# Two instead of three x tiles transposed on TensorE at the head of a gated attention/MLP kernel, and another order of the first loads

## The chip, the cores and the metric

The kernel runs on one core of a Trainium2 chip. The metric is the device time of one execution in microseconds (us). The engines are TensorE (PE in the profile, its weight loads PEld), VectorE (DVE), ScalarE (ACT), GpSimd (POOL) and SyncE (SP). DMAs are issued by SP, ACT or POOL and carried by 16 DMA engines; each issuing engine has a ring of its own (in the profile q1 holds what SP issued, q10 what ACT issued).

## The reference

```
x = A_x                                     # 1 x 2048 x 512, bf16
qkv = x @ wqkv                              # split into q, k, v; 32 heads of 16
phi(t) = where(t > 0, t + 1, exp(t)) + 1e-6
kv = phi(k)^T v ; z = sum over s of phi(k)  # per head, linear attention
a  = (phi(q) kv / (phi(q) z + 1e-6)) @ wo
h  = layernorm(x)                           # over the 512 features
u  = gelu(h^T w1 + b1)                      # mixes the 2048 tokens, 2048 -> 1792
b  = (u w2 + b2)^T                          # 1792 -> 2048
g  = sigmoid(sum(x * gate_w))               # one gate per token
out = g * a + (1 - g) * b
```

## The kernel before, in words

x is handled as 16 tiles of 128 tokens x 512 features. It is needed in two layouts: `xs` with the tokens on the partitions (plain loads, line 126), and `xT` with the features on the partitions. TensorE multiplies with the contraction on the partitions, so K and Q, which contract over features, need `xT`; the layernorm, the token mixing and the product x^T phi(K) need `xs`.

The work on TensorE comes in stages, and the order on every engine is written out by hand (`manual_schedule`): each engine does its instructions in the order in which the program names them, and waits where an input is not there.

1. Six matmuls on a constant (`warm_up`, tile `wps`).
2. The head: the first `HEADS` tiles of x are transposed on TensorE. `transpose_part` multiplies 128-column pieces of `xs` with an identity matrix into a PSUM bank `pt`, and `copy_part` copies them into `xT` on VectorE (line 212) or ScalarE (line 210). The other tiles come into `xT` by DMA transposes straight from memory (`load_xT`, line 132, issued by SP).
3. K for one tile (`k_part`, tile `kacc`): four matmuls of 512 columns, one for each 128 features, each with one piece of `Wk` (`wk_sb`). Then `k_phi`: ScalarE takes the exponential (line 216), VectorE finishes phi in two instructions (lines 217 and 220) into `pk`.
4. From tile 4 on, K of tile t alternates with `g_tile(t - 4)`: four matmuls into the four banks `gacc`, from `xs` and `pk` of the earlier tile. Layernorm statistics (line 240), their use (line 256) and small loads go between.
5. Token mixing with W1 (`uacc`), interleaved at first with Q (`qacc`), then the attention's small products, then for each output tile `aps` and `yps`, and the store.

W1 arrives in four chunks (`w1c`), W2 later in the same buffers.

What sets the order around the change: SP issues x tile 0, x tile 1, piece 2 of Wk, and then the DMA transposes. Ahead of those stands an instruction on VectorE at line 156 which copies eight columns of `xs` tile 0 into `xT` where the first DMA transpose will write. Its values are overwritten; but the transpose has to wait for it, and it waits for x tile 0. ACT issues the first two pieces of Wk in one load, then x tile 2, then piece 3 of Wk. Each DMA is told of by one of eight semaphores, used in turn; a DMA which takes one over is issued only after its earlier user has landed.

Of the kernel before, what the change touches and what calls it, by code (L numbers as in the profile page):

```python
# [15 lines left out]
def kernel(  # L16
# [13 lines left out]
    nc = tc.nc  # L30
    P = nc.NUM_PARTITIONS
# [8 lines left out]
    NT = S // P  # L40
    ND = D // P
# [15 lines left out]
    w1_view = B_w1.rearrange("(t p) f -> p t f", p=P)  # L57
# [8 lines left out]
    def keep(shape, dtype, name):  # L66
        return persist.tile(shape, dtype, name=name, tag=name)

    def bank(name, dtype=FP32):
        return ps.tile([P, SC], dtype, name=name, tag="bank")  # L70

    xs = keep([P, NT, D], BF16, "xs")
    hs = keep([P, NT, D], BF16, "hs")
    xT = keep([P, ND, S], BF16, "xT")
# [34 lines left out]
    def mm(o, lhsT, rhs, start, stop, **kw):  # L109
        nc.tensor.matmul(o, lhsT=lhsT, rhs=rhs, start=start, stop=stop, **kw)  # L110
# [14 lines left out]
    def load_x(q, t0, n):  # L125
        q.dma_start(out=xs[:, t0 : t0 + n, :], in_=x_view[:, t0 : t0 + n, :])

    def load_wk(q, k, n):
        q.dma_start(out=wk_sb[:, k : k + n, :], in_=wqkv_view[:, k : k + n, D : 2 * D])

    def load_xT(t0, n):
        nc.sync.dma_start(
            out=xT[:, :, t0 * P : (t0 + n) * P], in_=X[t0 * P : (t0 + n) * P, :], transpose=True
        )

    load_x(nc.sync, 0, 1)
    load_wk(nc.scalar, 0, 2)
    load_x(nc.sync, 1, 1)
    load_x(nc.scalar, 2, 1)
    load_wk(nc.sync, 2, 1)  # L140
    load_wk(nc.scalar, 3, 1)
    nc.vector.memset(ones_f[:], 1.0)
    nc.vector.memset(mhalf[:], -0.5)
    nc.gpsimd.memset(ident[:], 0.0)
    nc.gpsimd.affine_select(
        out=ident[:], in_=ident[:], compare_op=ALU.not_equal, fill=1.0, base=0,
# [5 lines left out]
        out=maskQ[:], in_=maskH[:].rearrange("p (a m) -> p m a", m=2), op=ALU.max, axis=AX.X  # L152
    )
    nc.gpsimd.memset(brow[:], 0.0)

    nc.vector.tensor_copy(
        out=xT[:, :, 3 * P : 3 * P + 2],
        in_=xs[:, 0, 0 : 2 * ND].rearrange("p (k c) -> p k c", k=ND),
    )
    load_xT(3, 2)  # L160
    load_xT(5, 3)
    load_x(nc.sync, 3, 1)
    load_x(nc.sync, 4, 4)
    for t0, n in ((8, 4), (12, 4)):
        load_xT(t0, n)
        load_x(nc.sync, t0, n)
# [2 lines left out]
    for c, (j0, nb) in enumerate(w1_chunks):  # L169
        w = wpool.tile([P, NT, FB * P], BF16, name="w1c", tag="wc")  # L170
        w1c.append(w)
        for t0 in range(0, NT, 8) if c == 0 else (0,):
            t1 = t0 + 8 if c == 0 else NT
            nc.sync.dma_start(
                out=w[:, t0:t1, : nb * P], in_=w1_view[:, t0:t1, j0 * P : (j0 + nb) * P]
            )
        if c == 0:
            nc.sync.dma_start(out=wv_sb[:], in_=wqkv_view[:, :, 2 * D : 3 * D])
            nc.sync.dma_start(out=wo_sb[:], in_=wo_view)
# [21 lines left out]
    def transpose_part(t, k0, k1):  # L201
        pt = pts[t, k0, k1] = bank("pt")
        for k in range(k0, k1):
            mm(pt[:, k * P : (k + 1) * P], xs[:, t, k * P : (k + 1) * P], ident[:], True, True)

    def copy_part(t, k0, k1, on_act):
        src = pts.pop((t, k0, k1))[:, k0 * P : k1 * P].rearrange("p (k s) -> p k s", k=k1 - k0)
        dst = xT[:, k0:k1, t * P : (t + 1) * P]
        if on_act:
            nc.scalar.activation(out=dst, in_=src, func=ACT.Copy)  # L210
        else:
            nc.vector.tensor_copy(out=dst, in_=src)

    def phi(dst, acc):
        e = work.tile([P, SC], BF16, name="e", tag="e", bufs=6)
        nc.scalar.activation(out=e[:], in_=acc[:], func=ACT.Exp)  # L216
        nc.vector.tensor_scalar(  # L217
            out=e[:], in0=e[:], scalar1=1.0, scalar2=PHI_EPS, op0=ALU.min, op1=ALU.add
        )
        nc.vector.scalar_tensor_tensor(  # L220
            out=dst, in0=acc[:], scalar=0.0, in1=e[:], op0=ALU.max, op1=ALU.add
        )
# [3 lines left out]
    def k_part(t, ks):  # L226
        if t not in kaccs:
            kaccs[t] = bank("kacc")
        for k in ks:
            mm(  # L230
                kaccs[t][:], xT[:, k, t * P : (t + 1) * P], wk_sb[:, k, :],
                k == 0, k == ND - 1,
            )

    def k_phi(t):
        phi(pk[:, t, :], kaccs.pop(t))
# [46 lines left out]
    def ln_step(u):  # L283
        ln_stats(u)
        if u % TPC == TPC - 1:
            ln_rstd(u // TPC)

    HEADS = 3
    for k0, k1 in ((0, 1), (1, 2), (2, ND)):
        transpose_part(0, k0, k1)  # L290
        copy_part(0, k0, k1, k0 == 2)
    k_part(0, range(2))
    for k0, k1 in ((0, 1), (1, 2), (2, ND)):
        transpose_part(1, k0, k1)
    for k0, k1 in ((0, 2), (2, ND)):
        transpose_part(2, k0, k1)
    copy_part(1, 0, 1, False)
    copy_part(1, 1, 2, True)
    copy_part(2, 0, 2, False)
    copy_part(2, 2, ND, True)  # L300
    copy_part(1, 2, ND, False)
    k_part(1, range(2))
    k_part(2, range(2))
    ln_step(0)
    for t in range(HEADS):
        k_part(t, (2,))
    for t in range(HEADS):
        k_part(t, (3,))
        k_phi(t)
    ln_step(1)  # L310
    LAG = 4
    LN_LAG = 5
    APPLY = 10
    for t in range(HEADS, NT):
        k_part(t, range(ND))
# [144 lines left out]
    for j in range(NB0, NF):  # L460
        c, jj = divmod(j, FB)
# [30 lines left out]
        out=gg[:], in0=gth[:], scalar1=0.5, scalar2=0.5, op0=ALU.mult, op1=ALU.add  # L492
    )
    nc.vector.tensor_scalar(
        out=c1[:], in0=gth[:], scalar1=-0.5, scalar2=0.5, op0=ALU.mult, op1=ALU.add
# [3 lines left out]
    for t in range(NT):  # L499
        c, tl = divmod(t, TPC)  # L500
        aps = bank("aps")
        for j in range(ND):
# [3 lines left out]
            out=a_sc[:], in_=aps[:], func=ACT.Identity,  # L506
            scale=gg[:, t : t + 1], bias=c2[:, t : t + 1],
        )
        for c0, W in ((0, 2 * P), (2 * P, P), (3 * P, P)) if t == NT - 1 else ((0, D),):
            cs = slice(c0, c0 + W)  # L510
            yps = bank("yps")
            for f in range(NF):
# [6 lines left out]
                out=ot[:, :W], in0=yps[:, :W], scalar=c1[:, t : t + 1], in1=a_sc[:, cs],  # L519
# [35 lines left out]
```

## Time and profile before

| | |
|---|---|
| runs, median (lowest to highest) | 162.54 us (162.47 to 163.53) |
| profiled execution, span of its instructions | 160.8 us |
| the same execution's own time | not recorded apart from the span; the median is 1.74 us above the span |
| TensorE busy | 156.3 us, 97% |
| granted TensorE clock after the first 4 us | full, to the end |

The span runs from the first to the last instruction. What lies around it (start and end of the execution) is in the times of the runs and not in the span.

The loads of the head, by the trace: issued, landed (the last completion mark), all in us from the span's start.

| load | issued by | size | issued | landed |
|---|---|---|---|---|
| x tile 0 | SP | 128 KB | 0.81 | 3.23 |
| Wk pieces 0, 1 | ACT | 256 KB | 0.80 | 3.94 |
| x tile 1 | SP | 128 KB | 1.27 | 4.32 |
| x tile 2 | ACT | 128 KB | 1.30 | 4.70 |
| Wk piece 2 | SP | 128 KB | 1.73 | 5.15 |
| Wk piece 3 | ACT | 128 KB | 1.82 | 6.03 |
| xT tiles 3, 4 (transpose) | SP | 256 KB | 3.45 | 7.21 |
| xT tiles 5 to 7 (transpose) | SP | 384 KB | 4.83 | 8.71 |
| x tile 3 | SP | 128 KB | 6.70 | 10.21 |
| x tiles 4 to 7 | SP | 512 KB | 7.32 | 11.60 |
| xT tiles 8 to 11 (transpose) | SP | 512 KB | 7.79 | 13.51 |
| W1 chunk 0, two halves | SP | 2 x 1 MB | 17.04, 19.71 | 26.11, 29.42 |

### The profile page before, as it was taken

Reading aid. Unit: us, or ns where it says so; the run is one execution under the profiler, and the core shown is the slowest. Engines: PE = TensorE matmul, PEld = TensorE weight load, DVE = VectorE, ACT = ScalarE, POOL = GpSimd, SP = SyncE. Lnnn points to the kernel's source line nnn. Section 1 sums busy time; section 2 is a strip of 40 time slices with the busy share of each in tenths; the row PEclk is TensorE's granted clock in tenths of the full one; section 3 lists DMA queues with packets and bytes.
Section 4 is the critical chain, followed back from the end, with each engine's and each line's share of the span. In section 5 each row is a group of like instructions: output and inputs, shape, how many; then the busy total and the mean of one; then the engine's idle time right before and its main releaser. Section 6 shows DMA issues by size and latency. Waiting matters only on the chain.

```text
span 160.8 us, 2241 instructions
## 1 busy us (share of the span) xinstructions
PE 156.3 (97%) x826; PEld 72.6 (45%) x840; DVE 124.8 (78%) x276; ACT 72.8 (45%) x114; POOL 7.3 (5%) x17
## 2 busy tenths in 40 slices
PE   7999999999999999999999999999999999999993
PEld 2444444444444444444444444444444444444462
DVE  1599999769999998756999999676999999711122
ACT  3552476654978483059873330237433442111110
POOL 3000332002020000000000000000000000000000
PEclk9999999999999999999999999999999999999999
DMA  5999999999970007600930689501000001110001
GB/s 165 229 235 238 274 335 295 359 348 348 335 177 0 0 0 236 225 0 5 335 120 2 186 270 288 169 33 37 33 33 33 33 33 60 47 60 33 33 33 33
DMA packets 29369, 22.94 MB, mean 143 GB/s; under 512 B 7824, under 2 KB 29328, under 8 KB 29360
## 3 DMA queue, kind: packets, MB, share of 16 engines
q1 hardware_dynamic: 28400, 21.89, 46.1%
q10 hardware_dynamic: 848, 0.79, 1.4%
q0 software_dynamic: 112, 0.14, 0.7%
q8 instruction: 6, 0.10, 0.3%
q14 instruction: 3, 0.02, 0.0%
HBM read 19.01 MB, written 2.10 MB: 131 GB/s over the span
## 4 chain that ended last, share of the span: by engine, by line
PE 94%; DVE 3%; issue 1%; ACT 0%
PE uacc L110 30%; PE yps L110 30%; PE aps L110 9%; PE qacc L110 8%; PE gacc L110 8%; PE kacc L110 7%; PE wps L110 2%; DVE pk L220 1%; DVE e L217 1%; DVE stats L240 0%; ACT e L216 0%; PE kvps L110 0%; PE pt L110 0%; PE w2ps L110 0%; DVE ot L518 0%
## 5 line engine op out<-in xcount | busy, mean ns | idle before, releaser
L110 PE MATMUL uacc<-hs,w1c 128*128 128x512 bf16 (+1 forms) x230 | 51.2, 379 | 0.3 <-issue 0.2
L110 PE MATMUL yps<-uT,w2c 128*128 128x512 bf16 (+2 forms) x247 | 50.8, 355 | 0.3
L110 PEld LDWEIGHTS <-w2c 128*128 128x128 bf16 x252 | 23.6, 98 | 25.2
L110 PEld LDWEIGHTS <-w1c 128*128 128x128 bf16 (+1 forms) x233 | 21.8, 98 | 26.0 <-issue 0.2
L505 ACT ACTIVATE a_sc<-aps,c,gg 128x512 f32<-128x512 f32 x16 | 12.4, 774 | 31.2 <-PE aps L110 15.5
L518 DVE SCALAR_TENSOR_TENSOR ot<-yps,c,a_sc 128x512 bf16<-128x512 f32 (+2 forms) x18 | 12.3, 688 | 15.4 <-PE yps L110 11.7
L339 ACT ACTIVATE uT<-uacc,bcol 128x512 bf16<-128x512 f32 x14 | 9.3, 686 | 17.5 <-PE uacc L110 17.4
L110 PE MATMUL aps<-W2sb,pqT 128*128 128x512 bf16 x63 | 16.4, 379 | 0.1
L110 PE MATMUL qacc<-xT,wq_sb 128*128 128x512 bf16 x61 | 16.1, 379 | 0.2
L110 PE MATMUL kacc<-wk_sb,xT 128*128 128x512 bf16 x63 | 15.9, 380 | 0.2
L404 DVE STREAM_TRANSPOSE zT<-pz 128x512 f32<-128x512 f32 x16 | 11.3, 705 | 6.0 <-ACT pz L403 6.0
L110 PE MATMUL gacc<-pk,xs 128*128 128x512 bf16 x63 | 15.6, 379 | 0.0
L256 ACT ACTIVATE hs<-xs,nmr,rstd 128x512 bf16<-128x512 bf16 x16 | 12.8, 805 | 2.3 <-DVE nmr L250 2.3
L403 ACT ACTIVATE pz<-pqT,zcol 128x512 f32<-128x512 bf16 x16 | 11.4, 714 | 4.8 <-DVE ot L518 4.7
L216 ACT ACTIVATE e<-kacc 128x512 bf16<-128x512 f32 x16 | 9.2, 596 | 9.7 <-PE kacc L110 9.6
L216 ACT ACTIVATE e<-qacc 128x512 bf16<-128x512 f32 x16 | 9.5, 594 | 7.7 <-PE qacc L110 7.7
L413 DVE STREAM_TRANSPOSE rex<-rd 128x512 bf16<-128x512 bf16 x16 | 11.4, 712 | 0.6
L220 DVE SCALAR_TENSOR_TENSOR pk<-kacc,e 128x512 bf16<-128x512 f32 x16 | 11.1, 692 | 0.6
L220 DVE SCALAR_TENSOR_TENSOR pqT<-qacc,e 128x512 bf16<-128x512 f32 x16 | 11.1, 691 | 0.6
L406 DVE TENSOR_REDUCE den<-zT 128x32 f32<-128x512 f32 x16 | 11.0, 686 | 0.6
L110 PEld LDWEIGHTS <-xs 128*128 128x128 bf16 x76 | 7.2, 100 | 8.3 <-DMA xs<-in_A_x_dram 0.6
L240 DVE BATCH_NORM_STATS2 stats<-xs 128x6 f32<-128x512 bf16 x16 | 10.9, 683 | 0.0
(59 smaller groups left out, 99.3 us busy)
## 6 DMA issues: line engine op xcount, KB each, us to landing
w2c<-in_B_w_dram SPq DMA_DIRECT2D x8, 896.0 KB, 5.8
w1c<-in_B_w_dram SPq DMA_DIRECT2D x2, 2048.0 KB, 15.7
w1c<-in_B_w_dram SPq DMA_DIRECT2D x3, 1024.0 KB, 9.7
out_dram<-ot SPq DMA_DIRECT2D x13, 128.0 KB, 1.7
xs<-in_A_x_dram SPq DMA_DIRECT2D x3, 512.0 KB, 4.5
wq_sb<-in_A_wqkv_dram SPq DMA_DIRECT2D x1, 512.0 KB, 6.6
wv_sb<-in_A_wqkv_dram SPq DMA_DIRECT2D x1, 512.0 KB, 10.4
wo_sb<-in_A_wo_dram SPq DMA_DIRECT2D x1, 512.0 KB, 9.1
```

The source lines that it names most:

```text
L110: nc.tensor.matmul(o, lhsT=lhsT, rhs=rhs, start=start, stop=stop, **kw)
L216: nc.scalar.activation(out=e[:], in_=acc[:], func=ACT.Exp)
L220: nc.vector.scalar_tensor_tensor(out=dst, in0=acc[:], scalar=0.0, in1=e[:], op0=ALU.max, op1=ALU.add)
L240: nc.vector.bn_stats(out=stats[:], in_=xs[:, t, :])
L256: nc.scalar.activation(out=hs[:, t, :], in_=xs[:, t, :], func=ACT.Identity, scale=rstd[:, t : t + 1], bias=nmr[:, t : t + 1],)
L339: nc.scalar.activation(out=uT[:, j, :], in_=acc[:], func=ACT.Gelu_apprx_tanh, bias=bcol[:, j : j + 1])
L403: nc.scalar.activation(out=pz[:], in_=seg, func=ACT.Copy, scale=zcol[:, j : j + 1])
L404: nc.vector.transpose(out=zT[:], in_=pz[:])
L406: nc.vector.tensor_reduce(out=den[:], in_=zT[:].rearrange("p (a d) -> p a d", d=HEAD), op=ALU.add, axis=AX.X)
L413: nc.vector.transpose(out=rex[:].rearrange("p (a d) -> p a d", d=HEAD), in_=rd[:].unsqueeze(2).to_broadcast([P, SC // HEAD, HEAD]),)
L505: nc.scalar.activation(out=a_sc[:], in_=aps[:], func=ACT.Identity, scale=gg[:, t : t + 1], bias=c2[:, t : t + 1],)
L518: nc.vector.scalar_tensor_tensor(out=ot[:, :W], in0=yps[:, :W], scalar=c1[:, t : t + 1], in1=a_sc[:, cs], op0=ALU.mult, op1=ALU.add,)
```

## The change

The head transposes two tiles on TensorE instead of three. Their two loads go first, one on SP's ring and one on ACT's, and Wk follows in four pieces of 128 KB, two on each ring. Behind them on SP stand the DMA transposes of tiles 2 and 3, one tile each, then those of tiles 4 and 5 and of tiles 6 and 7, and then one plain load of tiles 2 to 7. The copy at line 156 is gone, so that no DMA transpose waits for x tile 0 by that way. The first chunk of W1 comes in one load of 2 MB. On TensorE all eight transposes come first, then pieces 0 and 1 of K for both tiles, then pieces 2 and 3; the layernorm statistics of tile 0 come behind phi of both tiles.

```diff
     load_x(nc.sync, 0, 1)
-    load_wk(nc.scalar, 0, 2)
-    load_x(nc.sync, 1, 1)
-    load_x(nc.scalar, 2, 1)
+    load_x(nc.scalar, 1, 1)
+    load_wk(nc.sync, 0, 1)
+    load_wk(nc.scalar, 1, 1)
     load_wk(nc.sync, 2, 1)
     load_wk(nc.scalar, 3, 1)
+    load_xT(2, 1)
+    load_xT(3, 1)
...
-    nc.vector.tensor_copy(
-        out=xT[:, :, 3 * P : 3 * P + 2],
-        in_=xs[:, 0, 0 : 2 * ND].rearrange("p (k c) -> p k c", k=ND),
-    )
-    load_xT(3, 2)
-    load_xT(5, 3)
-    load_x(nc.sync, 3, 1)
-    load_x(nc.sync, 4, 4)
+    load_xT(4, 2)
+    load_xT(6, 2)
+    load_x(nc.sync, 2, 6)
...
-        for t0 in range(0, NT, 8) if c == 0 else (0,):
-            t1 = t0 + 8 if c == 0 else NT
-            nc.sync.dma_start(
-                out=w[:, t0:t1, : nb * P], in_=w1_view[:, t0:t1, j0 * P : (j0 + nb) * P]
-            )
+        nc.sync.dma_start(out=w[:, :, : nb * P], in_=w1_view[:, :, j0 * P : (j0 + nb) * P])
...
-    HEADS = 3
+    HEADS = 2
     for k0, k1 in ((0, 1), (1, 2), (2, ND)):
         transpose_part(0, k0, k1)
-        copy_part(0, k0, k1, k0 == 2)
-    k_part(0, range(2))
-    for k0, k1 in ((0, 1), (1, 2), (2, ND)):
+    for k0, k1 in ((0, 2), (2, ND)):
         transpose_part(1, k0, k1)
-    for k0, k1 in ((0, 2), (2, ND)):
-        transpose_part(2, k0, k1)
-    copy_part(1, 0, 1, False)
-    copy_part(1, 1, 2, True)
-    copy_part(2, 0, 2, False)
-    copy_part(2, 2, ND, True)
+    copy_part(0, 0, 1, False)
+    copy_part(0, 1, 2, True)
+    copy_part(0, 2, ND, False)
+    copy_part(1, 0, 2, True)
     copy_part(1, 2, ND, False)
-    k_part(1, range(2))
-    k_part(2, range(2))
+    for ks in (range(2), range(2, ND)):
+        for t in range(HEADS):
+            k_part(t, ks)
+            if ks[-1] == ND - 1:
+                k_phi(t)
     ln_step(0)
-    for t in range(HEADS):
-        k_part(t, (2,))
-    for t in range(HEADS):
-        k_part(t, (3,))
-        k_phi(t)
     ln_step(1)
```

## The prediction

> **What bounds the kernel.** I read the page first: how busy TensorE is, in which slices, and what the chain that ended last is made of.
>
> ```profile
> span 160.8 us, 2241 instructions
> ...
> PE 156.3 (97%) x826; PEld 72.6 (45%) x840; DVE 124.8 (78%) x276; ACT 72.8 (45%) x114; POOL 7.3 (5%) x17
> ...
> PE   7999999999999999999999999999999999999993
> ...
> PE 94%; DVE 3%; issue 1%; ACT 0%
> ```
>
> TensorE is busy in every slice and is 94% of the chain. Next, the busy time of the engines stage by stage, and the waits of TensorE over the whole run (engine, line, what it waited for, total, times, longest):
>
> ```profile
> 0.84:3.36 2.52, 2.52 (x6) 0.79 (x7) 0.36 (x4) 1.06 (x1) 1.14 (x6) 1.00 0.53 167
> 3.36:4.06 0.70, 0.63 (x6) 0.37 (x5) 0.41 (x3) 0.46 (x3) 0.00 (x0) 1.00 1.13 368
> 4.06:5.13 1.07, 1.07 (x11) 0.73 (x11) 0.49 (x3) 0.63 (x2) 0.00 (x0) 1.00 0.79 259
> 5.13:9.02 3.89, 3.89 (x19) 1.65 (x19) 2.73 (x8) 2.34 (x5) 0.00 (x0) 1.00 1.01 190
> 9.02:32.33 23.31, 23.20 (x107) 10.58 (x108) 21.53 (x54) 12.63 (x21) 3.82 (x5) 1.00 1.08 297
> ```
>
> ```profile
> PE wps L110 <- PEq L539: 0.8, 1, 0.8
> PE uacc L110 <- issue: 0.2, 1, 0.2
> ```
>
> The first number after the window is its length, the second TensorE's busy time: from 5.13 us on they are the same, and no DMA or other engine holds TensorE up. A matmul of 512 columns starts every 0.216 us (18 in the 3.89 us from 5.13). So the end of the kernel is the start of the head plus all work behind it, and the change is worth what it moves the first `g_tile` matmul, which starts at 9.02 now: everything from there on is the same on TensorE. It is moved back only if an input of a later stage comes late.
>
> The head itself, in order of time:
>
> ```profile
> 3.36 0.63 PE L110 MATMUL pt<-ident,xs 128*128 128x128 bf16 x4
> ...
> 4.06 0.62 PE L110 MATMUL kacc<-wk_sb,xT 128*128 128x512 bf16 x2
> 4.52 0.62 PE L110 MATMUL pt<-ident,xs 128*128 128x128 bf16 x8
> 5.13 4.06 PE L110 MATMUL kacc<-wk_sb,xT 128*128 128x512 bf16 x18
> 9.02 1.03 PE L110 MATMUL gacc<-pk,xs 128*128 128x512 bf16 x4
> ```
>
> The 5.66 us from 3.36 to 9.02 are, by starts: 4 transposes at 0.107 us (the array's clock is granted in full only from 4.14), 0.27 us of waiting for the copy into `xT`, 2 K matmuls (0.46), 8 transposes at 0.057 (0.46), 0.15 us for the next copy, and 18 K matmuls (3.89).
>
> **The change on TensorE.** It has 8 transposes and 20 K matmuls before the first `g_tile`. The transposes start at 3.36 as now (behind `wps`; x tile 0 still leads SP's ring). Seven run at 0.107 and one at 0.057, to 4.17. The copies keep their durations: VectorE's first ends at 4.00, ScalarE's 128-column piece (0.28) at 4.11, ScalarE's 256-column piece of tile 1 (0.38) begins when the sixth transpose is through, about 4.24, and ends 4.63. So K starts at 4.20, and the third K matmul waits for that copy, to 4.67 instead of 4.63. Eight head matmuls then end at 4.67 + 6 x 0.216 = 5.97, tiles 2 to 4 at 5.97 + 12 x 0.216 = **8.56**. Without any late load the gain is 9.02 - 8.56 = 0.46 us: only 0.07 of it from transposes (0.88 us for twelve, 0.81 for eight, since seven of them now run before the clock is up), the rest from the waits on copies, 0.42 before and 0.07 now, which other transposes cover.
>
> **The loads.** The landings of before are spaced by bytes, not by ring: 384 KB at 3.94, 512 KB at 4.32, 640 KB at 4.70, 768 KB at 5.15, some 0.37 us for 128 KB. By position the new order gives x tile 1 at about 3.6 (needed 3.79), Wk pieces 0 to 3 at 3.94, 4.32, 4.70 and 5.15; needed at 4.20, 4.42, 5.10 and 5.32. The last is the doubtful one. Wk piece 3 of before, the load which the transposes overtook, had ten of its sixteen completion marks by 5.35 and the last at 6.03, 0.88 behind the load before it and not 0.4. The line-156 copy held the transposes to 3.45; now they are issued from 2.13 and stand directly behind Wk piece 2, while piece 3 is on the other ring. So I take its tail with it: 6.03 less one tile's 0.37 = 5.66. The ends are 5.15 and 6.03. At 5.66, K waits 0.34 us and tile 2 begins at 6.31.
>
> The Trainium skill, "DMA: Bandwidth & Descriptors", section on queues, rings and completion order, says that each DMA engine goes round between the queue rows that have work, packet batch by batch, which speaks against dropping the hold: transposes and Wk piece 3 would share the engines. By fair halves, the last 40 KB or so of piece 3 would cost only another 0.1 us, an estimate from that rule; the trace's 6.03 says that completion suffers more than the sharing.
>
> **The one-tile transposes.** No one-tile transpose is in this trace. The issue of the two- and three-tile ones took 1.335 and 1.817 us on SP, so 0.48 for a tile and 0.85 for a single one: SP issues tiles 2 and 3 at 2.13 and 3.0, tiles 4-5 at 3.9 (its reused semaphore is that of x tile 1, landed by then), tiles 6-7 at 5.2, the load of x tiles 2 to 7 at 6.6; it has no earlier duty. Landing: the two-tile transpose needed 3.76 us from issue and 2.37 from its first packet (4.84); the three-tile one landed 1.50 later, 0.50 for a tile. The first packet is now behind Wk piece 2, at about 4.35 (one x tile less than 4.70). Lower end for tile 2: at the steady 0.50 a tile, and the 0.6 from the last data packet to the completion mark, 5.5. Upper end: all that the two-tile one took, 6.72. I take the middle, 6.1, since the trace's burst is slow for its first microsecond, which a single tile pays too. That is before 6.31: **no wait of its own**. Tile 3 then lands near 6.7 (needed 7.17), tiles 4-5 near 7.75 (needed 8.04), 6-7 near 8.75 (needed 11.5).
>
> The same page, section on the anatomy of one DMA, has about 2.0 us fixed plus bytes at 436 GB/s for each DMA (a fit for another issuing path); for 128 KB that is 2.3 us, an estimate, and tile 2 would land at 4.4, with nothing to wait for. The trace's 3.76 for 256 KB speaks for the slower figures, which I use.
>
> **What else is moved.** x tiles 2 to 7 come as one load of 768 KB, first needed by `g_tile(2)` near 12.3. Its bytes start behind the transposes, about 8.0 as now; the 640 KB of before were down by 11.60, and 128 KB more at 0.37 gives 11.97 if the gap between the two loads of before stays, nearer 11.2 if one load closes it. Cover: 0.3 to 1.1 us. If it is gone, TensorE waits by the difference, upper bound about 0.5. The W1 chunk in one load lands near 29.4, the second half's time; first use is at 32.3, so 2.9 us of cover; wq lands at 23.05 for 33. VectorE loses the copy of line 156 and two of its five copies out of `pt`, ScalarE one of three; neither was what TensorE waited for later. VectorE does the statistics of tiles 0 and 1 (0.87 us each) before phi of tile 2, whose bank and product are needed at 11.7 and 12.3; it ends near 11.2. PSUM banks come free in time by the same 0.5 us.
>
> **Sum.** Gain 0.46, less 0.34 for Wk piece 3: first `g_tile` at 8.90 instead of 9.02, 0.12 us. Against the profiled execution 160.8 becomes 160.7; with the 1.74 us that lie between the span and the median, **162.4 us**. One per cent is 1.6 us, about what a measurement of this kernel can tell from no change.
>
> **Rivals.**
> - *All loads in time*: Wk piece 3 at 5.15 and tile 2 by 5.97. First `g_tile` 8.56, 162.1 us. For it: landings by bytes. Against: the tail to 6.03.
> - *The single-tile transposes land late*: tile 2 at 6.72 or after a second slow start for each DMA. K of tile 2 at 6.72 gives `g_tile` at 9.31, 0.29 later; with another 0.5 for a burst's start before tiles 4-5, 0.8. So 162.8 to 163.3. It loses against the present from a landing of tile 2 after 6.43. For it: the burst's first microsecond in the trace, where DMA is fully busy and moves 190 GB/s. Against: one stream of transposes follows another without a break (7.21 and 8.71).
> - *The transposes do not overlap*, each paying the 2.37 us anew: tiles 2, 3, 4-5 at 6.7, 9.1 and 11.5, first `g_tile` at 12.3, 3.3 us later, 165.9: slower, by over 1% from a loss of 1.6, that is, when tiles 4-5 land after 9.8. Against: 8.71 - 7.21 = 1.50 for three tiles shows overlap.
> - *x tiles 2 to 7 late for `g_tile(2)`*: up to 0.5 us, 162.9.
> - *The change does nothing measurable* is close to the forecast and counted there.
>
> **Chances.** Forecast (162.2 to 162.6) 0.46; all in time 0.15; late transposes 0.27; x tiles late 0.05; no overlap 0.07. The range 161.9 to 163.5 takes in the first four and the bounds of Wk piece 3 (5.15 to 6.03, 0.17 better to 0.37 worse). Faster by over 1% would need 1.6 us where TensorE has 0.5 to give: 0.02. Slower by over 1%: no overlap and something unseen, 0.09. Within 1%: 0.89.
>
> **What would show it.** Right: eight transposes without a break, a pause of some 0.3 us ended by Wk before the sixth K matmul, none ended by `xT`, first `g_tile` at 8.8 to 9.0, no idle TensorE after. Wrong: a wait of weight loads on the DMA of `xT` at tiles 2 to 4, or on `xs` at the third `g_tile`; a clock granted in full later than 4.1 us.

## The result

The changed kernel takes 163.56 us (median of 20 runs, 163.02 to 163.99); the kernel before, run beside it, 163.16 us (20 runs, 162.45 to 163.62). The ratio is 1.0032, 95% interval 1.0020 to 1.0044: slower by 0.52 us, with 0.33 to 0.72 as bounds (the two medians lie 0.40 us apart, inside these bounds). The forecast was 162.4 us, 0.12 us less than before.

The spread of the runs is part of the result. Six of the twenty runs of before lie between 162.45 and 162.59; none of the changed kernel's is below 163.02. At the other end, eight of the changed kernel's are longer than the longest of before. The median and the lowest of the three times of before in the table ahead were such low ones, and so was the profiled execution.

The page of the changed kernel, span and chain:

```profile
span 161.8 us, 2242 instructions
...
PE 90%; SPq 4%; DMA 4%; issue 0%; DVE 0%
PE uacc L110 30%; PE yps L110 30%; PE qacc L110 9%; PE aps L110 9%; PE gacc L110 8%; PE kacc L110 5%; DMA xs<-in_A_x_dram 4%; SPq L132 3%; SPq L129 1%; PE kvps L110 0%; SPq L126 0%; PE w2ps L110 0%; DVE ot L505 0%; PE pt L332 0%
```

SP's queue and a DMA of `xs`, which had no part in the chain before, have 8% of it now. The profiled execution took 163.57 us itself, 1.77 over its span. TensorE in order of time (start, length, line, operation; in brackets its idle time and what ended it):

```profile
3.56 1.04 PE L110 MATMUL pt<-ident,xs 128*128 128x128 bf16 x8
4.38 5.22 PE L110 MATMUL kacc<-wk_sb,xT 128*128 128x512 bf16 x20
9.44 1.03 PE L110 MATMUL gacc<-pk,xs 128*128 128x512 bf16 x4
...
12.03 1.03 PE L110 MATMUL kacc<-wk_sb,xT 128*128 128x512 bf16 x4
13.47 0.82 PE L110 MATMUL gacc<-pk,xs 128*128 128x512 bf16 x3 [0.41 <-DMA xs<-in_A_x_dram]
```

The third `g_tile` starts at 13.47 where its place was 12.90 (12.03 and four matmuls at 0.216), a wait of 0.57 us for the one load of x tiles 2 to 7; the bracket counts less, because the modelled end of the matmul before reaches into the gap. Before, it started at 12.47, with no wait ahead of it:

```profile
11.61 1.03 PE L110 MATMUL kacc<-wk_sb,xT 128*128 128x512 bf16 x4
12.47 1.03 PE L110 MATMUL gacc<-pk,xs 128*128 128x512 bf16 x4
```

The 1.0 us between 12.47 and 13.47 is the whole difference of the two spans. SP's queue shows why the load is late (start, length, line, DMA, count):

```profile
2.21 5.30 SPq L132 DMA_TRANSPOSE xT<-in_A_x_dram  x4
7.55 0.58 SPq L126 DMA_DIRECT2D xs<-in_A_x_dram  x1
8.18 5.00 SPq L132 DMA_TRANSPOSE xT<-in_A_x_dram  x1
```

The four transposes hold SP for 1.30, 1.26, 1.30 and 1.30 us: one tile costs it as much as two. The load goes out at 7.55 and lands at 13.42, 5.9 us later.

But in this execution the full clock came at 5.88, in the profile of before at 4.14. In the line at 4.38 the 20 K matmuls take 5.22 us; the first four start 0.427 apart and the later ones 0.216. (The clock column of the windows view reads 1.00 in these stretches too, since the trace's clock records begin only with the full clock; the spacing shows it.) Whether the change or chance moved it was the first question.

### The profile page after: what moved, and what is told of

Same layout as the page of the kernel before. It is cut to its first block, busy times and chain, and to the rows that moved or that the text cites. A ratio compares the mean times of both kernels' runs of the same rounds, so it can differ in the third digit from the quotient of the medians.

```text
span 161.8 us, 2242 instructions
## 1 busy us (share of the span) xinstructions
PE 157.8 (98%) x836; PEld 72.6 (45%) x836; DVE 124.3 (77%) x273; ACT 72.6 (45%) x113; POOL 7.3 (4%) x17
## 4 chain that ended last, share of the span: by engine, by line
PE 90%; SPq 4%; DMA 4%; issue 0%; DVE 0%
PE uacc L110 30%; PE yps L110 30%; PE qacc L110 9%; PE aps L110 9%; PE gacc L110 8%; PE kacc L110 5%; DMA xs<-in_A_x_dram 4%; SPq L132 3%; SPq L129 1%; PE kvps L110 0%; SPq L126 0%; PE w2ps L110 0%; DVE ot L505 0%; PE pt L332 0%
## 5 line engine op out<-in xcount | busy, mean ns | idle before, releaser
L110 PE MATMUL kacc<-wk_sb,xT 128*128 128x512 bf16 x64 | 16.5, 393 | 0.0
L209 ACT ACTIVATE e<-kacc 128x512 bf16<-128x512 f32 x16 | 9.4, 594 | 11.2 <-PE kacc L110 9.5
L210 DVE TENSOR_SCALAR e<-e 128x512 bf16<-128x512 bf16 x32 | 9.0, 281 | 4.1 <-ACT e L209 4.1
```

Source lines behind the costliest of these rows:

```text
L210: nc.vector.tensor_scalar(out=e[:], in0=e[:], scalar1=1.0, scalar2=PHI_EPS, op0=ALU.min, op1=ALU.add)
```

## Second profiles of both kernels

The same two kernels, profiled once more. The kernel before:

> The kernel before, a second profile. Theory 'phase': the moment when the array's clock is granted in full (4.14 us in one profile of before, 5.88 in that of the changed kernel) differs from execution to execution of the same kernel, so that it can lie anywhere from about 4 to 7 us here. Rival 'gap': the pause of 0.19 us ahead of the transposes of the changed kernel put it off; then it is 4.1 here again.

The changed kernel:

> The changed kernel, a second profile. Theory 'phase': another moment of the full clock than 5.88 us, and the third g_tile still at 13.4 to 13.5, since it waits for a load and not for TensorE; the span within 0.3 us of 161.8. Rival 'gap': full clock at 5.9 again.

The kernel before, second profile, TensorE in order of time; its span is 161.8 us, not 160.8:

```profile
4.07 1.02 PE L110 MATMUL kacc<-wk_sb,xT 128*128 128x512 bf16 x2
4.88 1.06 PE L110 MATMUL pt<-ident,xs 128*128 128x128 bf16 x8
5.74 4.40 PE L110 MATMUL kacc<-wk_sb,xT 128*128 128x512 bf16 x18
9.98 1.03 PE L110 MATMUL gacc<-pk,xs 128*128 128x512 bf16 x4
...
13.43 1.03 PE L110 MATMUL gacc<-pk,xs 128*128 128x512 bf16 x4
```

Full clock came at 6.44, and the third `g_tile` at 13.43 instead of 12.47. The order of the work is the same; only the array was slow for longer. The changed kernel, second profile:

```profile
3.58 0.73 PE L110 MATMUL pt<-ident,xs 128*128 128x128 bf16 x8
4.26 1.04 PE L110 MATMUL kacc<-wk_sb,xT 128*128 128x512 bf16 x4
5.45 2.94 PE L110 MATMUL kacc<-wk_sb,xT 128*128 128x512 bf16 x12 [0.15 <-DMA wk_sb<-in_A_wqkv_dram]
8.79 1.04 PE L110 MATMUL kacc<-wk_sb,xT 128*128 128x512 bf16 x4 [0.40 <-DMA xT<-in_A_x_dram]
...
13.52 1.04 PE L110 MATMUL gacc<-pk,xs 128*128 128x512 bf16 x4 [0.24 <-DMA xs<-in_A_x_dram]
```

Here the clock was early: from 3.87 the transposes start 0.056 apart instead of 0.107, and the four K matmuls at 4.26 start 0.22 apart. TensorE then waits at every load in turn. By matmul starts: 0.32 us for Wk piece 2 (landed 5.41), 0.19 for piece 3 (5.81), 0.57 for the transpose of tiles 4 and 5 (8.74), 0.40 for x tiles 2 to 7 (13.47). All of the early clock is lost, and the third `g_tile` starts at 13.52.

| | clock | third g_tile | span |
|---|---|---|---|
| before | early, 4.14 | 12.47 | 160.8 |
| before, second profile | late, 6.44 | 13.43 | 161.8 |
| changed | late, 5.88 | 13.47 | 161.8 |
| changed, second profile | early (no record; by the spacing, near 3.9) | 13.52 | 161.8 |

So the moment of the full clock varies between executions of one and the same kernel; that the changed kernel's pause of 0.19 us ahead of its transposes put it off is not needed, since its second profile had an early clock after a pause of 0.23 us, and before had a late one without any. In these four profiles the two kernels take the same time with a late clock; with an early one the kernel before gains about 1 us and the changed kernel nothing. That is not all of the 20 runs: the eight that are longer than any of before are not explained by it, and none of them was profiled. The Trainium skill, "TensorE: Matmul & The Clock Gate", Part 1, says that the activity window which decides is free-running and does not start with the kernel, so that the same kernel has different counts of slow matmuls. These runs agree that the moment varies: over all the kernels of this document, eleven of thirteen profiles recorded it, at 3.47 to 6.49 us, all with the first matmul at 0.84 or 0.85. That a free-running window is behind it no run here shows.

## One load cut off: x tile 2 alone

```diff
-    load_x(nc.sync, 2, 6)
+    load_x(nc.sync, 2, 1)
+    load_x(nc.sync, 3, 5)
```

> The changed kernel with its load of x tiles 2 to 7 cut in two: tile 2 alone, then tiles 3 to 7. Theory 'load': what the change loses is the wait of the third g_tile for that one load, which landed at 13.42 us where TensorE was ready at 12.90. Tile 2 alone then lands at about 11 (tile 3 of before, issued at 6.70, needed 3.5 us), tiles 3 to 7 at about 13.4 for a use near 14.6; no pause before any g_tile, span about 161.2 where the clock comes up as late as in the profile of the changed kernel (5.9 us), and a median 0.4 us below the changed kernel's, within 0.1% of before. Rival 'head': the loss is the later x tile 0 and the slow first K matmuls, and the wait only hides it; the median stays 0.3% over before.

Measured: ratio to before 1.0026 (1.0015 to 1.0036). x tile 2 landed at 11.13 and tiles 3 to 7 at 13.03, and no `g_tile` waits any more. Yet an earlier wait is now the one that counts:

```profile
4.31 4.37 PE L110 MATMUL kacc<-wk_sb,xT 128*128 128x512 bf16 x16
8.85 1.04 PE L110 MATMUL kacc<-wk_sb,xT 128*128 128x512 bf16 x4 [0.17 <-DMA xT<-in_A_x_dram]
9.72 1.03 PE L110 MATMUL gacc<-pk,xs 128*128 128x512 bf16 x4
...
13.17 1.03 PE L110 MATMUL gacc<-pk,xs 128*128 128x512 bf16 x4
```

K of tile 4 starts 0.33 us late by matmul starts, for a transpose that landed at 8.80. The third `g_tile` is 0.30 us earlier than in the changed kernel, not 0.57, and TensorE's last matmul 0.31 (the span is not shorter: in this execution 0.28 us more passed between that matmul and the end). Theory "load" misses its span and its time. The rival's number, 0.3% over before, is inside the interval, and by the times the edit is not shown to gain anything on the changed kernel's 1.0032. In the profile the third `g_tile` has moved, so the load is one cause, and a second wait stands close ahead of it.

## Two tiles in one transpose

```diff
-    load_xT(2, 1)
-    load_xT(3, 1)
+    load_xT(2, 2)
```

> The changed kernel with tiles 2 and 3 in one DMA transpose of two tiles instead of two of one tile. Theory 'issue': a one-tile transpose holds SP for as long as a two-tile one (1.30 and 1.26 us in the profile), so the load of x tiles 2 to 7 is issued at 6.25 instead of 7.55 and lands near 12.1, in time for the third g_tile (12.3 to 12.9); tile 2 lands near 6.0, before its use at 6.9. No wait left, median 0.4 us below the changed kernel's. Rival 'bytes': the load lands late because of the bytes ahead of it, the same in both; it lands near 13.2 and the median stays.

Measured: ratio 1.0015 (1.0000 to 1.0030). The load of x tiles 2 to 7 was issued at 7.18, not 6.25, because the next transpose now took 2.07 us on SP; it landed at 12.94, later than expected but 5.76 us after its issue, as in the changed kernel (5.87): this load lands earlier by about what its issue is earlier. Tiles 4 and 5 do not follow their issue in the same way: issued at 3.72 instead of 4.86, they landed at 8.24 instead of 8.35 (8.74 in the second profile). The ratio lies below the changed kernel's 1.0032, with overlapping intervals. In the profiled execution the clock came at 6.49, and no wait for any of these loads is left in it.

Both edits together:

> The changed kernel with both edits: tiles 2 and 3 in one transpose, and x tile 2 loaded alone ahead of tiles 3 to 7. Theory 'gates': the changed kernel is held by three sets of landings at fixed times (Wk pieces 2 and 3 at 5.4 to 5.8, transpose of tiles 4 and 5 at 8.4 to 8.8, x tiles 2 to 7 at 13.4), so that an early full clock is lost again. Here the last is gone (x tile 2 near 10.8) and the second is near 8.2; left are Wk and tile 2 (6.1 to 6.9). Ratio to before 1.000 to 1.0015, at or below the lower of the two single edits (1.0015). Rival 'one gate': only the load of x tiles 2 to 7 matters; then it is the same as x2_alone, 1.0026.

Measured: ratio 1.0005 (0.9985 to 1.0026), lowest run 162.35 us, lower than any run of before (162.45). It can't be told from before, and is not shown to differ from the two-tile transpose alone; its interval and the changed kernel's (1.0020 to 1.0044) barely overlap. By the point values each removed wait brings the kernel nearer to before, as "gates" had it. In its profile, with the clock at 3.93, one large wait is left, for Wk, whose piece 2 landed at 5.96 (5.37 in the changed kernel), with a smaller one for tile 2 behind it:

```profile
4.27 1.06 PE L110 MATMUL kacc<-wk_sb,xT 128*128 128x512 bf16 x4
6.00 3.84 PE L110 MATMUL kacc<-wk_sb,xT 128*128 128x512 bf16 x16 [0.67 <-DMA wk_sb<-in_A_wqkv_dram]
9.68 1.03 PE L110 MATMUL gacc<-pk,xs 128*128 128x512 bf16 x4
```

Another cut of the same transposes, one tile and then three:

```diff
-    load_xT(3, 1)
+    load_xT(3, 3)
...
-    load_xT(4, 2)
-    load_xT(6, 2)
-    load_x(nc.sync, 2, 6)
+    load_xT(6, 2)
+    load_x(nc.sync, 2, 1)
+    load_x(nc.sync, 3, 5)
```

> The changed kernel with transposes of tile 2 alone, tiles 3 to 5 in one, tiles 6 and 7 in one, and x tile 2 loaded alone. One transpose issue fewer on SP than in the changed kernel. Theory 'gates': tile 2 lands near 6.1, tiles 3 to 5 near 7.9, x tile 2 near 10.8; K of tile 3 waits for the three-tile transpose where the clock is early (ready at 7.1), 0.5 to 0.8 us; ratio 1.0005 to 1.002. Rival 'one gate': 1.0026 as x2_alone.

Measured: ratio 1.0032 (1.0017 to 1.0047). Tiles 3 to 5 landed at 8.31, and K of tile 3, which needs only the first of them, waited 0.76 us (8.36 instead of 7.60). The wait is as expected; the ratio is above what was expected of it.

## The hold put back, and the hold alone taken away

```diff
-    load_xT(2, 1)
-    load_xT(3, 1)
...
+    nc.vector.tensor_copy(
+        out=xT[:, :, 2 * P : 2 * P + 2],
+        in_=xs[:, 0, 0 : 2 * ND].rearrange("p (k c) -> p k c", k=ND),
+    )
+    load_xT(2, 1)
+    load_xT(3, 1)
     load_xT(4, 2)
```

> The changed kernel with the hold put back: VectorE copies eight columns of x tile 0 into xT where tile 2 will be transposed to, so that all DMA transposes are issued after x tile 0 has landed (near 3.6 instead of 2.2). Theory 'overtaking': without the hold the transposes delay the completion of Wk pieces 2 and 3 (5.4 and 5.6 to 5.8); with it they land at 4.8 and 5.3 or a little later. All later gates move 1.3 us back: tile 2 near 7.2, tiles 4 and 5 near 9.9, x tiles 2 to 7 near 14.8, so the third g_tile starts at 14.8 and the median is 1.0 to 1.3 us above the changed kernel's, ratio to before 1.009 to 1.012. Rival: Wk lands no earlier, it is late because of its place behind two x tiles on shared engines; the times of the gates are the same.

Measured: ratio 1.0128 (1.0101 to 1.0155), just above the 1.012 expected. TensorE:

```profile
7.77 1.04 PE L110 MATMUL kacc<-wk_sb,xT 128*128 128x512 bf16 x4 [0.18 <-DMA xT<-in_A_x_dram]
10.17 1.04 PE L110 MATMUL kacc<-wk_sb,xT 128*128 128x512 bf16 x4 [1.36 <-DMA xT<-in_A_x_dram]
...
15.01 0.39 PE L110 MATMUL gacc<-pk,xs 128*128 128x512 bf16 x1 [0.56 <-DMA xs<-in_A_x_dram]
```

The waits moved back as expected, by 1.4 to 1.5 us, and the time followed: the loads set it. The one-tile transposes held SP for 1.30 and 1.26 us here too, with no transpose ahead of the first. Tile 2 landed at 6.51, earlier than the 7.2 expected, but tiles 4 and 5 only at 10.13. Wk pieces 2 and 3 landed at 5.54 and 5.73, as late as without the hold, though the first transpose packet came only at 5.17 (4.21 in the changed kernel). So holding the transposes back to 3.76 does not bring these pieces forward, and theory "overtaking" misses. That the transposes have no part in it is not shown: in the three kernels whose first two transposes carry four tiles (two and two, or one and three) the pieces landed at 5.83 to 5.96 and 6.04 to 6.23, in the five profiles with one tile each and no hold at 5.37 to 5.65 and 5.60 to 5.92.

The other direction, the kernel before without the copy at line 156 and nothing else:

> The kernel before without the copy at line 156 alone: the transposes are issued near 2.2 instead of 3.3 to 3.5. Theory 'overtaking': Wk pieces 2 and 3 land later than the 5.15 to 5.6 and 5.9 to 6.0 of before, near 5.9 and 6.4; they are needed at 6.0 and 6.65 with an early clock, so three heads of K cover them and the transposes of tiles 3 and 4 land near 6.5, before their use; ratio 0.999 to 1.001. Rival: x tile 0 or the other early loads are slowed as well and the head starts later; ratio over 1.001.

Measured: ratio 1.0004 (0.9984 to 1.0023); its lowest run was 162.49. Wk pieces 2 and 3 landed at 5.38 and 5.59, where the two profiles of before have 5.15 and 6.03, and 5.62 and 5.89: piece 2 between them, piece 3 earlier than both. Dropping the hold is not shown to cost anything where three tiles of K stand on TensorE in front of the transposes' first use (tiles 3 and 4 landed at 6.50), and the later landings that "overtaking" expected did not come.

## A later head, and the order of the rings

Two more matmuls on a constant make TensorE later and move no load.

```diff
-    warm_up(6)
+    warm_up(8)
```

In the changed kernel:

> The changed kernel with eight instead of six matmuls on a constant at the start, which makes the head 0.4 to 0.85 us later on TensorE and moves no load. Theory 'gates': the third g_tile waits for x tiles 2 to 7, landed at 13.4 to 13.5, in any case, so the delay is taken out of the waits: median within 0.2 us of the changed kernel's, ratio to before 1.002 to 1.004. Rival 'work': the head's work on TensorE sets the time; the median rises by 0.4 to 0.85 us, ratio 1.0055 to 1.0085.

In the kernel before:

> The kernel before with the same two extra matmuls. Theory 'gates': no load holds TensorE there, so the whole delay goes to the end: 0.4 to 0.85 us more, ratio 1.0025 to 1.005. Rival: loads hold it as well, and the ratio is within 0.999 to 1.001.

Measured: 1.0039 (1.0024 to 1.0054) for the changed kernel, 0.0007 over its 1.0032, and 1.0023 (1.0005 to 1.0041) for the kernel before, 0.37 us, just under the 1.0025 expected. For the changed kernel the interval ends below the 1.0055 at which the rival "work" begins. The point values say that the changed kernel takes up most of the delay in its waits and the one before does not; the two intervals overlap, so by times alone that difference is not settled. The profiles agree with it. The third `g_tile` of the changed kernel, then of the kernel before:

```profile
13.60 1.04 PE L110 MATMUL gacc<-pk,xs 128*128 128x512 bf16 x4 [0.39 <-DMA xs<-in_A_x_dram]
...
12.85 1.03 PE L110 MATMUL gacc<-pk,xs 128*128 128x512 bf16 x4
```

The first still waits for x tiles 2 to 7 and is 0.13 us later than in the changed kernel, although its transposes start 0.65 us later; the second waits for nothing and is 0.38 us later than before, with transposes that start 0.49 us later.

```diff
-    load_x(nc.scalar, 1, 1)
-    load_wk(nc.sync, 0, 1)
+    load_wk(nc.scalar, 0, 1)
+    load_x(nc.sync, 1, 1)
```

> The changed kernel with x tile 1 second on SP and Wk pieces 0, 1 and 3 on ACT, as the order of the rings was before. Theory 'sharing': x tile 0 landed at 3.4 to 3.55 instead of 3.0 to 3.2 because x tile 1 is moved beside it; here it lands at 3.05 to 3.25 and the transposes of tile 0 start at 3.36, those of tile 1 wait for their load to 4.0 to 4.4. Wk piece 2 is now the third on SP, so the DMA transposes start no earlier. Theory 'gates' has the time unchanged by all that (third g_tile at 13.4, ratio 1.002 to 1.004). Rival: the head decides, and the ratio falls or rises by 0.002 or more.

Measured: ratio 1.0036 (1.0018 to 1.0053). The time is unchanged as "gates" had it, although tile 1's transposes now wait for their load; the load of x tiles 2 to 7 landed at 13.76 in this profile and the third `g_tile` started at 13.81, not 13.4. "Sharing" falls in the form that was given: x tile 0 landed at 3.46, not at 3.05 to 3.25. In all nine profiles with a load of 128 KB at the front of both rings it landed at 3.37 to 3.55, in the four with one 256 KB load of Wk in front on ACT at 3.03 to 3.23. Which difference between these two groups does it stays open.

## Why the prediction was wrong

**The starting point.** "The array's clock is granted in full only from 4.14": this was taken as a property of the kernel, and 160.8 us with it. It is one draw: a second profile of before has 6.44 and 161.8. Against the 20-run median of before, 163.16, the forecast's own gain of 0.12 would have been 163.0. That is 0.6 us of the distance to 163.56, and it has nothing to do with the change. The prediction named a later full clock as a sign of being wrong but gave it no price.

**"The change is worth what it moves the first `g_tile` matmul"**, since no DMA holds TensorE up: this is the step that failed. It is true of before, and the 0.46 us less of pure head was right in kind: without its waits for loads, the head of the second profile takes about 5.0 us from the first transpose to the first `g_tile` against 5.66, with a clock some 0.3 us earlier. But in the changed kernel TensorE waits for loads that the prediction had in time, above all the transpose of tiles 4 and 5 and x tiles 2 to 7; the terms below were mis-sized. For an early clock, which the forecast assumed, they add up: third `g_tile` forecast at 8.90 + 3.45 = 12.35, measured 13.52, 1.17 later.

| term | forecast | second profile of the changed kernel | error, us |
|---|---|---|---|
| x tile 0, start of the transposes | 3.36 | 3.58 | 0.22 |
| Wk pieces 2 and 3, wait | 0.34 | 0.32 + 0.19 | 0.17 |
| transpose of tiles 4 and 5, wait | 0 (landing 7.75) | 0.57 (landing 8.74) | 0.57 |
| x tiles 2 to 7, wait | 0 (landing 11.2 to 12.0) | 0.40 (landing 13.47) | 0.40 |
| head itself, shorter | | | -0.19 |

The last row is the remainder; most of it is that K began 0.68 us after the first transpose and not 0.84.

**The issue cost of a one-tile transpose** was too small. From 1.335 us for two tiles and 1.817 for three, a line gave 0.85 for one; it took 1.26 to 1.41 in the two profiles, as much as two tiles. Four transposes then held SP to 7.5 and 7.65 instead of 6.6, and tiles 4 and 5 were issued at 4.86 and 5.00 instead of 3.9. For x tiles 2 to 7 this is about 1 us of the late landing. For tiles 4 and 5 it is half of it at most: with two tiles in one transpose they were issued at 3.72, earlier than forecast, and landed at 8.24, still 0.49 us after the 7.75, where the changed kernel's two profiles are 0.60 and 0.99 us after it.

**The flow of the data** is the rest of that. The prediction had 0.50 us a tile as in one burst. With two-tile and three-tile transposes the five tiles of before took 3.2 and 3.4 us from the first packet to the last; in the changed kernel the first five took 4.1 and 4.3 and the six 4.8 and 5.1. Why it is slower is not shown. (The 190 GB/s that the prediction gives for the burst's first microsecond is the mean from 5.13 to 9.02; from 5 to 6 us it was 135.)

**x tiles 2 to 7** were the rival with a chance of 0.05 and at most 0.5 us; they cost 0.57 in the first profile and 0.40 in the second. Issue came 0.95 to 1.1 us late. From issue to landing it took 5.8 to 5.9 us, where 4.3 had been seen for 512 KB; x tile 2 alone took 3.6. A tile at the front of a load waits for the load's last: x tile 2 landed at 11.13 alone and at 13.42 as one of six.

**"Late transposes"**, at 0.27, named the right mechanism for tiles 4 and 5 but put its first part at tile 2, which landed at 5.99 and 6.05, about 0.1 us before the 6.1 that was taken. "No overlap" was wrong as expected: tile 3 landed 0.4 to 0.7 us behind tile 2.

**Wk piece 3** at 5.66 was right in size (5.60 and 5.81); its reason, the dropped hold, is not borne out: with the hold it came at 5.73. Piece 2, put at 4.70, came at 5.37 and 5.41. What keeps the last of these pieces back stays open. The covers named for W1 (landed 31.34, used at 33.34, 2.0 us instead of 2.9) and wq held.

## What to carry to other kernels

Where a kernel's start depends on something that varies by itself, here the array's clock, one profile of before is one draw: look at the spread of its times, and ask of a change whether it can still use the lucky draw. Work removed from a head gains nothing once fixed landing times stand behind it, and they show only when the covering work has gone. Before a DMA is cut finer to have its first piece sooner, ask what each piece costs to issue: here a one-tile transpose held SP as long as a two-tile one, about 1.3 us. The gain of joining two of them was smaller than that: the load behind them was issued 0.37 us sooner, since the next transpose then held SP for 2.07 us.

## What the runs showed that was not expected

- A DMA transpose of one 128 x 512 tile held SP's queue for 1.26 to 1.41 us, one of two tiles for 1.30 to 1.53, and for 2.07 and 2.08 where it came right behind another two-tile one early on.
- The full clock came between 3.47 and 6.49 us, with the first matmul at 0.84 or 0.85 in each profile; in the kernel before the difference between 4.14 and 6.44 was 0.96 us of span.
- No version tried beats before by more than the intervals allow: the nearest are both edits together (1.0005) and before without the hold (1.0004).
